# An attention and spectral-mixing kernel: the output stage with its two halves shared out anew between ScalarE, VectorE and GpSimd

## The chip, the cores and the metric

The kernel runs on one core of a Trainium2 chip. The metric is the device time of one execution in microseconds, told as the median of several runs; lower is better. A profile of one execution shows each engine: TensorE (PE, with its weight loads PEld), VectorE (DVE), ScalarE (ACT), GpSimd (POOL) and the queue engine SyncE (SP), which here only issues transfers.

## The reference

Two layers follow each other. The first is linear attention with a feature map of exponentials, for 8 batches, 8 heads, 576 tokens and 64 channels per head. Its output, with heads side by side, is `x` (8 x 576 x 512). The second is a spectral mix over the tokens and a projection:

```python
X = np.fft.rfft(x, axis=1)
Yr = einsum('bmd,mde->bme', Xr, w_r) - einsum('bmd,mde->bme', Xi, w_i)   # 64 modes
Yi = einsum('bmd,mde->bme', Xr, w_i) + einsum('bmd,mde->bme', Xi, w_r)
y = np.fft.irfft(Y, n=S, axis=1)
u = x + y
return (u + np.maximum(u @ w_ch, 0.0)).astype(np.float32)
```

`w_r` and `w_i` are 64 matrices of 512 x 512 in float32 each; they make up most of what is read.

## The kernel before

Tokens lie in 36 chunks `(bp, n)`: `bp` counts four pairs of batches and `n` nine groups of 128 rows. For `n` below 8 a chunk holds 128 tokens of one batch, and for `n` = 8 it holds 64 of each of the two batches. `chunk(bp, n)` is x of a chunk in bfloat16, `xw[:, bp, n]` is x times `w_ch`.

The mixing weights come in by 64 transfers on GpSimd's queue, in tiles `wt` of the pool `pw`, which has nine slots of one tag. `mix` multiplies one of them and adds up the spectrum `y` of eight modes for all batches; the modes are in eight groups `o`. When the last part of a group is there, `yst` is that group's spectrum, `zst` is `yst` times `w_ch`, got by transposing `yst` (`pt`, `yT`) and multiplying by `wchb` (`pz`). The output of a chunk is then the sum of two halves, both made in PSUM:

- p = x + (inverse table) x (spectrum y),
- q = xw + (inverse table) x (spectrum z), of which the Relu is taken,

and the result is p + relu(q). TensorE adds x or xw into a PSUM bank by a matmul with the identity `ident_b` (the "base"). Most of the spectrum (six of the eight groups) is added during the mix, while weights still arrive: `Absorb` adds it to x and xw in place. What is left comes after the last mix. Groups 6 and 7 are laid out in `yl`: 32 partitions each for y and z, twice, so that two chunks of a pair can be summed at once by matmuls of 32 rows with the table `CL` (method `late`). For chunks that are "early", group 6 has been absorbed too and only group 7 is left; it is read directly from `yst` and `zst` with the table `CM` and full-height matmuls (method `straight`). `put` sends `yst` and `zst` to `yl`; every copy is a DMA of 128 KB, here on SP for group 7.

The output stage begins with the last `mix` and is the class `Last`, one object for one chunk or a pair of chunks, in the order of the list `seq`. A pair goes through these steps:

- `base(1)`, then `late(1)` or `straight(1)`: q in two single banks (`pt`, pool `pst` with four banks);
- `relu`: ScalarE takes q out into `rl` (two buffers of the pool `pb`) or `rx` (a slot of `pw`), one chunk at a time;
- `base(0)`, then `late(0)` or `straight(0)`: p in a tile of two banks (`pp`, pool `pst2` with two such tiles);
- for five pairs (n = 8 and the pairs of bp = 2 in `added`, all `later`) the base of p is left out, and GpSimd adds x to `rx` instead, one chunk at a time;
- `store`: VectorE adds p and `rl` or `rx` into `of` (a slot of `pw`), and SP sends it out, 512 KB for a pair.

The first two chunks are handled singly: there ScalarE takes out p, and VectorE does the max and the add from q in one instruction. The last two, `(3, 6)` and `(3, 7)`, are single too, with tiles `ofr`. The order on every engine is the order in which the code calls it: `InOrder` keeps the recorded instructions in program order, so one late instruction holds all that follow it on its engine. The hand-written list `ahead` says how many pairs q runs ahead of p.

## Time and profile before

| | |
|---|---|
| median of 3 runs | 441.26 us |
| lowest and highest | 439.84 and 441.54 us |
| the profiled execution | 439.83 us |
| its span, first to last instruction | 438.0 us |
| TensorE, VectorE, ScalarE, GpSimd busy | 332.9, 294.0, 290.7, 111.7 us |
| mean granted TensorE clock | 0.905 |
| moved by the core's 16 DMA engines | 99.55 MB |

The page's slices cut the span in 40 parts of 11 us; a digit is the busy share in tenths. The chain that ended last is followed backwards from the last instruction, at each step to what released it. In lists of rows, each row is a start, a duration, an engine, an operation with the tile written and the tiles read, its size, and a count where equal neighbours are merged; in brackets stand the idle time in front of it and what ended that. A "landing" is the time from a transfer's issue to its completion.

### The profile page before, as it was taken

What the parts mean: (1) busy time and instruction counts of PE and PEld (TensorE: products, weight loads), DVE (VectorE), ACT (ScalarE), POOL (GpSimd) and SP (SyncE); (2) the same over time, 40 slices, a digit from 0 to 9 for tenths busy, and PEclk for the clock granted to TensorE, in tenths of its full rate; (3) what the DMA queues carried; (4) which work ended last, traced back from release to release, by engine and by line L of the source; (5) the groups of instructions that cost most, each with busy time, mean ns of one, the idle gap of its engine ahead of it and who ended that gap; (6) DMA issues with size and microseconds to landing.
All of it is one profiled execution on the core that took longest, in us unless ns stands there. A gap on an engine that the chain in (4) does not pass through costs nothing.

```text
span 438.0 us, 10095 instructions
## 1 busy us (share of the span) xinstructions
PE 332.9 (76%) x4209; PEld 198.5 (45%) x4209; DVE 294.0 (67%) x581; ACT 290.7 (66%) x472; POOL 111.7 (25%) x150
## 2 busy tenths in 40 slices
PE   2677667678697686787796877935779998997993
PEld 1345555455465454554554554612335554333320
DVE  6758677665776777887877778723773334785784
ACT  3787796776987977986977778600444442764781
POOL 6232132113211212222222221211101211682082
PEclk9979898789988989998987998875899999999996
DMA  9999999999999999999999999999999999996787
GB/s 217 209 211 211 238 213 236 237 213 248 227 211 239 226 229 230 238 215 235 231 218 239 210 262 212 213 212 212 213 215 222 223 219 222 212 219 147 258 358 292
DMA packets 51838, 99.55 MB, mean 227 GB/s; under 512 B 2512, under 2 KB 13648, under 8 KB 51792
## 3 DMA queue, kind: packets, MB, share of 16 engines
q0 software_dynamic: 45088, 85.27, 99.4%
q1 hardware_dynamic: 6544, 13.57, 8.8%
q8 instruction: 33, 0.54, 0.5%
q14 instruction: 13, 0.11, 0.1%
q10 hardware_dynamic: 160, 0.07, 0.1%
HBM read 163.64 MB, written 9.44 MB: 395 GB/s over the span
## 4 chain that ended last, share of the span: by engine, by line
ACT 28%; PE 27%; DMA 24%; DVE 12%; issue 7%; POOL 1%; POOLq 0%; ACTq 0%; DVEq 0%
DMA wt<-in_moe_w_r_dram 16%; PE one L37 14%; ACT AQ L37 12%; ACT AB L37 8%; PE two L37 8%; DMA wt<-in_moe_w_i_dram 8%; DVE m L37 6%; PE pt L37 3%; ACT qT L37 3%; ACT XT L37 3%; DVE mk L37 2%; PE pp L37 2%; DVE xs L37 1%; DVE yacc L37 1%; DVE of L37 1%
## 5 line engine op out<-in xcount | busy, mean ns | idle before, releaser
L37 ACT ACTIVATE AQ<-two 128x1024 bf16<-128x1024 f32 x64 | 80.6, 1350 | 2.7 <-PE two L37 2.6
L37 ACT ACTIVATE AB<-two 128x1024 bf16<-128x1024 f32 x64 | 62.9, 1059 | 3.0 <-DVE mk L37 2.7
L37 ACT CAST xw<-pt 128x512 bf16<-128x512 f32 x50 | 29.4, 587 | 47.7 <-PE pt L37 47.7
L37 DVE TENSOR_REDUCE m<-two 128x8 f32<-128x1024 f32 x32 | 39.2, 1224 | 21.9 <-PE two L37 21.8
L37 DVE TENSOR_REDUCE mk<-two 128x8 f32<-128x1024 f32 x32 | 38.9, 1218 | 8.7 <-PE two L37 8.7
L37 POOL DMA_DIRECT2D wt<-in_moe_w_i_dram x28 | 20.9, 748 | 91.2 <-PE pt L37 37.2
L37 PE MATMUL two<-w2blk,qT 128*128 128x256 bf16 x128 | 23.7, 318 | 25.3 <-ACT AQ L37 14.8
L37 DVE TENSOR_TENSOR va<-vn,ee 128x1152 bf16<-128x1152 f32 x32 | 42.0, 1356 | 0.0
L37 PE MATMUL pt<-wchb,xT 128*128 128x512 bf16 x136 | 37.0, 397 | 5.6 <-DVE xT L37 4.5
L37 POOL DMA_DIRECT2D wt<-in_moe_w_r_dram x30 | 22.3, 744 | 63.9 <-PE one L37 27.6
L37 PEld LDWEIGHTS <-xs 128*128 128x128 bf16 x624 | 31.6, 103 | 12.2 <-issue 6.4
L37 PE MATMUL one<-wt,XT 128*32 128x512 bf16 x304 | 27.3, 446 | 10.3 <-DMA wt<-in_moe_w_i_dram 4.6
L37 ACT COPY qT<-one 128x512 bf16<-128x512 bf16 (+1 forms) x32 | 19.0, 642 | 24.1 <-PE one L37 24.0
L37 PE MATMUL two<-qT,w2blk 128*128 128x512 bf16 x64 | 27.3, 427 | 9.3 <-ACT AQ L37 9.3
L37 PEld LDWEIGHTS <-qT 128*128 128x128 bf16 x144 | 15.2, 108 | 40.8 <-issue 37.1
L37 PEld LDWEIGHTS <-XT 128*32 128x32 bf16 x512 | 14.7, 149 | 35.2 <-issue 24.4
L37 DVE TENSOR_TENSOR xs<-one,rd 128x384 bf16<-128x384 f32 x48 | 26.8, 558 | 1.6
L37 PEld LDWEIGHTS <-AQ 128*128 128x128 bf16 x512 | 24.3, 107 | 7.7 <-issue 4.0
L37 PE MATMUL one<-kvz,AQ 128*128 128x65 bf16 x512 | 27.0, 207 | 0.9 <-ACT qT L37 0.8
L37 PE MATMUL two<-mT,minus 96*128 96x512 bf16 x64 | 27.5, 430 | 0.0
L37 POOL DMA_DIRECT2D kb<-in_k_dram x16 | 11.4, 712 | 60.4 <-PE one L37 51.1
L37 DVE COPY xT<-pt 128x512 bf16<-128x512 bf16 x36 | 15.2, 421 | 17.0 <-PE pt L37 17.0
(143 smaller groups left out, 712.6 us busy)
## 6 DMA issues: line engine op xcount, KB each, us to landing
wt<-in_moe_w_r_dram POOLq DMA_DIRECT2D x30, 1024.0 KB, 27.5
wt<-in_moe_w_i_dram POOLq DMA_DIRECT2D x28, 1024.0 KB, 28.7
out_dram<-of SPq DMA_DIRECT2D x16, 512.0 KB, 3.2
vn<-in_v_dram POOLq DMA_DIRECT2D x13, 576.0 KB, 24.6
kb<-in_k_dram POOLq DMA_DIRECT2D x16, 288.0 KB, 19.5
qb<-in_q_dram POOLq DMA_DIRECT2D x16, 288.0 KB, 18.6
xs<-in_moe_w_i_dram POOLq DMA_DIRECT2D x2, 1024.0 KB, 23.2
vn<-in_v_dram SPq DMA_DIRECT2D x3, 576.0 KB, 5.2
```

The source lines that it names most:

```text
L37: ins = f(*args, **kwargs)
```

## The change

The class `Last` gives way to a class `Pair`, and the calls after the last mix to a list of words, `plan`. All 36 chunks are handled in 18 pairs. Each pair has two sides: "e", taken out by ScalarE into `rl`, and "d", read by VectorE. The table `pairs` says for each pair whether its sums are direct (`straight`), whether ScalarE takes out q with Relu (`relu` true; VectorE then adds p) or p as it is (VectorE then does max and add from q), and whether GpSimd adds x to what ScalarE took out (`pooled`; then the base of p is left out). Eight pairs are pooled.

- A word of `plan` such as `eb34` means: side e, base, pair "34", both chunks. The letters are b for a base, s for a direct sum, l for a late sum; a fifth character picks one chunk. `mix`, `T0`, `T1`, `z0a`, `z0b`, `z1` are places in the last mix and channel product at which the list stops and goes on.
- Three pairs (00, 02, 06) are direct; before it was all of bp = 0 with n below 8. The tables and rows of `Absorb` follow that (`direct`). The chunks are no longer sorted.
- For direct pairs the add is done, and stored, chunk by chunk. All other adds are one instruction for both chunks. `rl` and `of` both come from `pw`.
- Of the two copies of the last `zst` to `yl`, the one for s = 3 is issued on GpSimd's queue.
- Both copies of the last transposed `yst` are VectorE's.

```diff
+    pairs = {
+        "00": (((0, 0), (0, 1)), True, False, False),
+        "02": (((0, 2), (0, 3)), True, False, True),
+        "06": (((0, 6), (0, 7)), True, True, True),
+        "34": (((3, 4), (3, 5)), False, False, False),
...
+        "n0": (((0, 8), (1, 8)), False, False, True),
...
+        "24": (((2, 4), (2, 5)), False, True, False),
...
+        "36": (((3, 6), (3, 7)), False, True, False),
+    }
+    plan = (
+        "eb000 db020 db000 db001 mix db021 T0 es021 T1 z0a es000 z0b z1 eb001 es020 es001 "
+        "ds000 ds001 eb060 es060 ds020 eb061 es061 ds021 eb34 el34 ds060 ds061 eln0 db34 eb04 "
+        "el04 dl34 db04 eb30 dl04 el14 el30 dbn0 dln0 eb24 db30 dl30 el22 el24 db14 dl14 db24 "
+        "el20 dl24 db22 el12 dl22 eb10 db20 dl20 el10 el32 db10 dl10 eb26 db12 dl12 el26 ebn1 "
+        "db26 dl26 eln1 db32 dl32 eb16 dbn1 dln1 el16 db16 eb36 dl16 el36 db36 dl36").split()
...
-            self.early = bp == 0 and n < 8
+            self.early = (bp, n) in direct
...
-    chunks.sort(key=lambda c: c not in added)
...
-                (pool if o == 6 else sp).dma_start(yl[r:r + 16], src)
+                (pool if o == 6 or s == 3 else sp).dma_start(yl[r:r + 16], src)
...
+        def keep(self, a):
...
+            if self.relu:
+                act.activation(rl, self.e[a], ACT.Relu)
+            else:
+                act.activation(rl, self.e[a], ACT.Copy)
+            if self.pooled:
+                x = rl.rearrange("p (g e) -> p g e", g=4)
+                pool.tensor_tensor(out=x, in0=x, in1=chunk(*self.items[a]), op=ALU.add)
+
+        def add(self, a):
+            rl, d, o = self.rl[:, a], self.d[:, a], self.o[:, a]
+            if self.relu:
+                dve.tensor_tensor(out=o, in0=d, in1=rl, op=ALU.add)
+            else:
+                dve.scalar_tensor_tensor(out=o, in0=d, scalar=0.0, in1=rl, op0=ALU.max,
+                                         op1=ALU.add)
...
-                if h:
+                if h or end:
                     dve.tensor_copy(yT[h], pt[h])
                 else:
                     act.copy(yT[h], pt[h])
```

## The prediction, made before the changed kernel was run

> **What bounds the kernel now.** I read the page's slices first, then the stage in windows, the chain that ended last, the engines' rows in order of time, and the DMA views.

> ```profile
> DMA  9999999999999999999999999999999999996787
> GB/s 217 209 211 211 238 213 236 237 213 248 227 211 239 226 229 230 238 215 235 231 218 239 210 262 212 213 212 212 213 215 222 223 219 222 212 219 147 258 358 292
> ```

> The transfers are full until the last weights (402.13 us in the chain, which is DMA for 35 us before that). Nothing the engines do earlier counts; the stage from 402 to 438 us does. There the windows show the bound moving:

> ```profile
> core 0: us, PE busy (x) PEld busy (x) DVE busy (x) ACT busy (x) POOL busy (x), PEclk, DMA share, GB/s
> ...
> 418.00:422.00 4.00, 4.00 (x25) 1.13 (x24) 3.58 (x3) 3.48 (x7) 3.71 (x4) 1.00 0.71 289
> ...
> 426.00:430.00 4.00, 3.26 (x20) 0.96 (x18) 3.46 (x3) 2.72 (x6) 3.47 (x4) 1.00 1.00 392
> 430.00:434.00 4.00, 1.57 (x4) 0.23 (x3) 2.52 (x3) 0.00 (x0) 0.04 (x1) 0.51 0.98 383
> ```

> TensorE is full to 428 while the stores leave DMA time unused (0.71 in 418 to 422); at the end TensorE is idle half the time and the stores are full. The chain's end tells why it still takes until 433.25:

> ```profile
> 427.10 0.59 ACT rx L37
> ...
> 427.77 1.16 POOL rx L37
> ...
> 430.07 1.24 DVE of L37
> ...
> 431.35 0.55 PE pp L37
> 431.89 0.67 issue
> 432.56 0.69 DVE ofr L37
> ```

> The last pairs go one after another: a Relu, two GpSimd adds (to 430.04), a VectorE add that frees a bank, two matmuls at a granted clock of about a half (0.58 us a row where it was 0.38), the last add. The single-step costs:

> ```profile
> 410.70 0.59 PE L37 MATMUL pt<-xw,ident_b 128*128 128x512 bf16 x2
> 411.23 0.39 PE L37 MATMUL pt<-yl,CL 32*128 32x512 bf16 x2
> 411.55 0.60 PE L37 MATMUL pt<-xw,ident_b 128*128 128x512 bf16 x2
> ...
> 406.43 1.29 DVE L37 SCALAR_TENSOR_TENSOR ofr<-pp,rl 128x512 f32<-128x512 f32 x2 [0.76 <-ACT rl L37]
> 408.41 2.36 DVE L37 TENSOR_TENSOR of<-pp,rl 128x1024 f32<-128x1024 f32 x2 [0.69 <-ACT rl L37]
> ...
> 419.95 4.64 POOL L37 TENSOR_TENSOR rx<-rx,xs 128x512 f32<-128x512 f32 x4 [0.29 <-ACT rx L37]
> ```

> Full-height matmuls start 0.43 apart per two, 0.216 each (407.25, 407.68, 408.11 and on). Into a run of 32-row matmuls and out again costs 0.53 + 0.32 where two full matmuls alone cost 0.43: such a run costs 0.42.

> **The change, part by part.**

> *Ahead of 402 us.* Chunks are no longer sorted, and six instead of eight are "direct". The idle time in front of the last mix (TensorE 1.55, VectorE 2.93, ScalarE 3.22 us) covers it: 0. Without that cover each microsecond would count.

> *TensorE's sum.* Before: 57 identity matmuls after the last mix (36 for xw, 26 for x, five ahead), 16 direct ones, 17 low runs, about five extra steps inside them (tile widths change at 421.2, 423.8, 425.0, 427.3: 0.33 each), 0.87 for the channel product, 0.25 for transposes: 12.3 + 3.5 + 7.1 + 1.5 + 1.1 = 25.5 us from 403.36. Less the two last singles (1.3), that gives 427.6; the trace has 428.9, so 1.3 us were waits. After: eight pairs instead of five get x from GpSimd, so x needs 20; 52 identity matmuls remain (11.2), 12 direct (2.6), again 17 low runs by the list (7.1), two changes of width (0.7), four places where two sets of the same rows follow each other (0.9), and 1.1: 23.6 us, to 427.0. With the same waits, 428.4.

> [...]

> *VectorE.* Before and after 36 chunk adds; now six of 512 and fifteen of 1024. First add at 406.43 as before: its ScalarE half is earlier, and zst later by only 0.15 (worked below). Ten of the fifteen wide ones (those where ScalarE takes out p) use the max-add form, which the trace shows at 512 alone: 0.60 apart, like the plain add. At 1024 it lies between the plain one's 1.14 to 1.18 apart and 1.29 for two narrow ones; I take 1.16, since at 512 the two forms agree. 6 x 0.60 + 15 x 1.16 = 21.0: 427.4 if never idle. TensorE's 428.4 ends later: last sum out 428.6, last add 429.8 (now 433.25).

> *ScalarE.* 36 takes at 0.52 and the zst copy, 19 us of 25: free. Both transposed copies go to VectorE (0.29 for 0.37) and one direct matmul stands between them; the product still ends about 405.1. But two takes (404.1 to 405.25) now precede zst, which starts 405.27 for 405.10: 0.15.

> *GpSimd.* 16 adds at 1.14 plus one copy issue 0.55: 18.8 us from 404.7, to 423.5. VectorE wants the last of them (pair 32) four adds before its end, at about 424.7. Cover of 1.2 us; see the first rival. [...]

> *The zst copy on GpSimd's queue.* Two zst copies used to go out on SP at 405.73 and 406.32, landing 3.4 and 3.6 later. Now one goes to GpSimd, behind its first add: issued 405.9. The list needs it for the run "el04 dl34": three matmuls, zst at 405.8, eight (407.5), two and a run (408.4), two and a run (409.2), four: 410.2. No row shows GpSimd's queue empty late in the kernel. Bounds: 3.4 (SP's rows) and 19.2; the nearest with nothing ahead is the first load:

> ```profile
> kb<-in_k_dram POOLq DMA_DIRECT2D x1, 288.0 KB, 6.6
> ...
> yl<-yst POOLq DMA_DIRECT2D x2, 128.0 KB, 19.2
> ...
> yl<-yst SPq DMA_DIRECT2D x2, 128.0 KB, 3.5
> ```

> kb is twice as large and ran beside other loads, the 19.2 stood behind weights; same size and route as SP's, so I take 4.3, nearer to SP's 3.5: 410.2, no cost. SP, relieved of one issue, has 21 stores of 0.55 in 24 us: free.

> [...]

> *Tiles.* rl and of now share eight slots (nine less yl), four pairs of about 1.2 us. A store that lands 4.8 after its issue holds its slot almost that long; 0 to 0.5 us at the end, where the stores bind anyway.

> *The stores.* Eighteen times 512 KB at 410 GB/s is 1.28 each, 23.0 in all. First store issued 407.15 as before; its landing took 3.2 of which 0.64 its bytes, so never idle the last lands at 407.15 + 2.56 + 23.0 = 432.7. From VectorE: 429.85 + 3.0 (an unqueued 512 KB) = 432.9. Two bounds so close queue on each other: 433.4. From 423.3 on, stores landed 4.2 to 4.9 after issue, not 3.0. The DMA view of 424 to 426 shows what shared the engines, an instruction fetch of 16 KB:

> ```profile
> q8 instruction: 1, 0.02, 4.4%
> ...
> out_dram<-of SPq DMA_DIRECT2D x2, 512.0 KB, 4.8
> ```

> TensorE's program is about as long, so it should come again; 1.1 to 1.8 late, take 1.4: 434.8. Last landing to end of span was 1.2 (436.8 to 438.0): **436.0, that is 2.0 us less**. The profiled run was 439.83 around its 438.0, 1.4 below the median 441.26 (runs 439.84 to 441.54). I predict **439.3** for the median. Half a percent, 2.2 us, is about what a measurement of this kernel can tell from no change.

> **The rivals.**

> *GpSimd's adds set VectorE's pace.* For: 18.8 us of work with 1.2 of cover, and before it idled 0.29, 0.36 and 0.53 between pairs waiting for Relus. Eight such gaps of 0.35 make 2.8: pair 32 ready at 426.3, VectorE 1.6 late, ends 431.4: gain 0.4, **440.9**. Against: the list puts pooled pairs well ahead. The same comes part way if max-adds at 1024 take 1.29 (10 x 0.13 = 1.3).

> *Slower: the zst copy lands late.* From 410.2 on, each microsecond holds TensorE, and everything in order behind it, for one; ScalarE and VectorE run dry with pair 06. At kb's 6.6 it lands 412.5: 2.3 lost, nothing gained, **441.5**. Past 8.5 after issue the kernel is over 0.5% slower; halfway between 6.6 and 19.2, at 12.9, it would be 8.6 - 2.0: **447.9**; at 9.5, **444.5**. Against: empty queue, small copy.

> **How the numbers follow.** Forecast case 0.58: from 1 to 3.3 us gained (438.0 if VectorE is never idle and the fetch costs 1.1, up to 440.3), 0.37 of it past 0.5%, 0.21 within. Adds rival 0.15, within. Copy rival 0.27: 0.10 within, 0.17 slower. So 0.37, 0.46, 0.17. The range leaves out most of the slow copy and a little below: 438.0 less 0.6 for the spread of medians, 437.4, to 442.5, with the copy 7.6 late.

> **What would show it.** Right: adds on VectorE with gaps under 0.5 us, last ending near 430; DMA share 1.0 from about 413; no serial GpSimd step in the chain's last 5 us; TensorE's last matmul near 428. Wrong: VectorE idle at 410 to 413 with TensorE waiting for the yl copy; VectorE waiting for GpSimd on rl more than 1 us in all; wide max-adds over 1.2 apart; a fall in the granted clock ahead of 428.

## The result, and the profile after

| | before | after |
|---|---|---|
| median of 22 runs | 440.13 us | 439.06 us |
| lowest and highest | 439.11 and 442.14 us | 437.69 and 440.18 us |
| the profiled execution | 439.83 us | 438.27 us |
| its span | 438.0 us | 436.4 us |
| first matmul of the last mix | 402.17 us | 402.45 us |
| first add of the stage begins | 406.43 us | 406.91 us |
| last add ends | 433.25 us | 430.46 us |
| last store lands | 436.82 us | 435.16 us |

The ratio of the times, with its 95% interval, is 0.9968 [0.9955, 0.9981], a gain of 1.4 us with an interval from 0.8 to 2.0; the two medians by themselves lie 1.1 apart. That is real, but within the half percent that the prediction called no change; the forecast was 439.3.

The last mix waits for the last weights, and these came 0.28 us later in the profile of after. Times marked "+" below are therefore counted from the first matmul of the last mix, so that the stage itself is compared: the span ends at +35.87 before and +33.94 after, 1.93 us less.

The page of after, the DMA rows of its slices:

```profile
DMA  9999999999999999999999999999999999998697
GB/s 214 209 212 210 238 212 237 235 214 241 235 211 239 219 229 237 238 210 239 224 224 238 210 262 212 212 212 213 212 216 223 220 223 222 212 219 176 226 393 297
```

Of the stage's three slices, the first moves 226 GB/s for 258 before and the second 393 for 358: fewer bytes at first, then the stores come closer together. The windows of after:

```profile
core 0: us, PE busy (x) PEld busy (x) DVE busy (x) ACT busy (x) POOL busy (x), PEclk, DMA share, GB/s
418.00:422.00 4.00, 3.96 (x23) 1.11 (x22) 3.56 (x4) 3.40 (x7) 4.00 (x5) 1.00 1.01 406
422.00:426.00 4.00, 4.00 (x26) 1.14 (x24) 3.92 (x4) 2.38 (x5) 2.78 (x3) 1.00 1.02 404
426.00:430.00 4.00, 2.88 (x19) 0.82 (x18) 3.61 (x4) 2.17 (x4) 0.00 (x0) 1.00 1.00 396
430.00:434.00 4.00, 0.00 (x0) 0.00 (x0) 0.47 (x1) 0.00 (x0) 0.00 (x0) 0.80 0.91 361
```

In 418 to 422 the stores now fill the DMA engines (1.01, before 0.71). GpSimd is done before 426. The stretch from 430 holds only the end of one add and the stores; before, it held four matmuls at half clock and 2.5 us of VectorE. TensorE's last row, and the end of the chain of waits of after (start, duration, what):

```profile
428.49 0.39 PE L37 MATMUL pp<-yl,CL 32*128 32x512 bf16 x2
```

```profile
427.69 0.32 PE pp L37 x2
428.01 0.09 PE pt L37 x2
428.10 0.01 issue
428.11 0.82 DVE of L37
428.93 0.29 issue
429.22 1.25 DVEq L1032
```

The serial steps of before (a Relu, two GpSimd adds, an add that frees a bank, two matmuls) are gone. From 416.4 the chain runs along TensorE to 428.1, and it ends with two adds on VectorE, one right behind the other. VectorE's rows of after, in order of time, tell where it waited (in brackets the idle time in front and what ended it):

```profile
406.91 2.72 DVE L37 SCALAR_TENSOR_TENSOR of<-pp,rl 128x512 f32<-128x512 f32 x4 [0.88 <-PE pp L37]
...
410.55 0.69 DVE L37 TENSOR_TENSOR of<-pp,rl 128x512 f32<-128x512 f32 x1 [0.33 <-POOL rl L37]
...
412.76 4.74 DVE L37 SCALAR_TENSOR_TENSOR of<-pp,rl 128x1024 f32<-128x1024 f32 x4 [0.30 <-PE pt L37]
...
420.35 1.22 DVE L37 SCALAR_TENSOR_TENSOR of<-pp,rl 128x1024 f32<-128x1024 f32 x1 [0.31 <-POOL rl L37]
...
428.11 2.35 DVE L37 TENSOR_TENSOR of<-pp,rl 128x1024 f32<-128x1024 f32 x2 [0.38 <-PE pt L37]
```

No gap between the adds exceeds 0.4 us. Before, the longest two were waits for TensorE's half p:

```profile
413.10 3.79 DVE L37 TENSOR_TENSOR of<-pp,rl 128x1024 f32<-128x1024 f32 x3 [0.92 <-PE pp L37]
...
418.12 2.52 DVE L37 TENSOR_TENSOR of<-pp,rl 128x1024 f32<-128x1024 f32 x2 [1.23 <-PE pp L37]
```

Between the adds VectorE idles 1.86 us in all, where it was 5.04.

### The profile page after: what moved, and what is told of

It is laid out like the page before. It is cut to its first block, busy times and chain, and to the rows that moved or that the text cites. A ratio compares the mean times of both kernels' runs of the same rounds, so it can differ in the third digit from the quotient of the medians.

```text
span 436.4 us, 10049 instructions
## 1 busy us (share of the span) xinstructions
PE 322.8 (74%) x4160; PEld 195.8 (45%) x4203; DVE 293.8 (67%) x583; ACT 290.0 (66%) x471; POOL 118.9 (27%) x157
## 4 chain that ended last, share of the span: by engine, by line
ACT 27%; PE 24%; DMA 24%; DVE 14%; issue 7%; POOL 2%; DVEq 0%; POOLq 0%; ACTq 0%
DMA wt<-in_moe_w_r_dram 16%; PE one L37 13%; ACT AQ L37 12%; ACT AB L37 9%; DMA wt<-in_moe_w_i_dram 8%; PE two L37 8%; DVE m L37 6%; ACT qT L37 3%; ACT XT L37 3%; PE pp L37 2%; DVE mk L37 2%; PE pt L37 2%; DVE xs L37 1%; DVE yacc L37 1%; DVE mT L37 1%
## 5 line engine op out<-in xcount | busy, mean ns | idle before, releaser
L37 ACT ACTIVATE AQ<-two 128x1024 bf16<-128x1024 f32 x64 | 80.5, 1346 | 2.9 <-PE two L37 2.8
L37 ACT ACTIVATE AB<-two 128x1024 bf16<-128x1024 f32 x64 | 62.9, 1058 | 3.2 <-DVE mk L37 3.0
L37 ACT CAST xw<-pt 128x512 bf16<-128x512 f32 x50 | 29.4, 587 | 48.2 <-PE pt L37 48.2
L37 DVE TENSOR_REDUCE m<-two 128x8 f32<-128x1024 f32 x32 | 39.1, 1223 | 20.3 <-PE two L37 20.2
L37 POOL DMA_DIRECT2D wt<-in_moe_w_i_dram x28 | 20.9, 748 | 97.2 <-PE pt L37 42.1
L37 DVE TENSOR_REDUCE mk<-two 128x8 f32<-128x1024 f32 x32 | 38.9, 1218 | 8.6 <-PE two L37 8.6
L37 DVE TENSOR_TENSOR va<-vn,ee 128x1152 bf16<-128x1152 f32 x32 | 42.0, 1355 | 0.0
L37 PE MATMUL two<-w2blk,qT 128*128 128x256 bf16 x128 | 21.7, 298 | 27.2 <-ACT AQ L37 15.0
L37 PE MATMUL pt<-wchb,xT 128*128 128x512 bf16 x127 | 35.6, 394 | 7.3 <-DVE xT L37 6.0
L37 POOL DMA_DIRECT2D wt<-in_moe_w_r_dram x30 | 22.3, 745 | 62.4 <-PE one L37 27.0
L37 PEld LDWEIGHTS <-xs 128*128 128x128 bf16 x624 | 31.5, 103 | 12.2 <-issue 6.4
L37 ACT COPY qT<-one 128x512 bf16<-128x512 bf16 (+1 forms) x32 | 19.0, 642 | 24.7 <-PE one L37 24.6
L37 PE MATMUL one<-wt,XT 128*32 128x512 bf16 x304 | 26.9, 440 | 10.8 <-DMA wt<-in_moe_w_i_dram 5.1
L37 PEld LDWEIGHTS <-qT 128*128 128x128 bf16 x144 | 14.6, 102 | 41.9 <-issue 38.8
L37 PEld LDWEIGHTS <-XT 128*32 128x32 bf16 x512 | 14.9, 149 | 35.3 <-issue 24.1
L37 PE MATMUL two<-mT,minus 96*128 96x512 bf16 x64 | 27.8, 434 | 3.2 <-issue 1.1
L37 PEld LDWEIGHTS <-AQ 128*128 128x128 bf16 x512 | 24.7, 109 | 7.9 <-issue 4.1
L37 PE MATMUL one<-kvz,AQ 128*128 128x65 bf16 x512 | 27.4, 209 | 0.9 <-ACT qT L37 0.8
L37 DVE TENSOR_TENSOR xs<-one,rd 128x384 bf16<-128x384 f32 x48 | 26.8, 557 | 1.6
L37 POOL DMA_DIRECT2D kb<-in_k_dram x16 | 11.4, 712 | 57.3 <-PE one L37 46.5
L37 DVE COPY xT<-pt 128x512 bf16<-128x512 bf16 x36 | 15.2, 421 | 17.0 <-PE pt L37 17.0
L37 DVE RECIPROCAL rd<-one 128x6 f32<-128x6 f32 x48 | 9.4, 195 | 24.7 <-PE one L37 24.3
## 6 DMA issues: line engine op xcount, KB each, us to landing
out_dram<-of SPq DMA_DIRECT2D x15, 512.0 KB, 4.0
vn<-in_v_dram POOLq DMA_DIRECT2D x13, 576.0 KB, 25.2
kb<-in_k_dram POOLq DMA_DIRECT2D x16, 288.0 KB, 20.5
qb<-in_q_dram POOLq DMA_DIRECT2D x16, 288.0 KB, 19.4
```

The lines of the kernel that those rows point to most:

```text
L37: ins = f(*args, **kwargs)
```

## The experiments

Every ratio is to the kernel before, run on the same chip, with its 95% interval; the kernel after stands at 0.9968.

**What sets the pace after: TensorE's sum or GpSimd's adds.** In `unpool3`, pairs 20, 12 and 32 get x from TensorE again.

```diff
-        "20": (((2, 0), (2, 1)), False, False, True),
+        "20": (((2, 0), (2, 1)), False, False, False),
...
-            "el20 dl24 db22 el12 dl22 eb10 db20 dl20 el10 el32 db10 dl10 eb26 db12 dl12 el26 ebn1 "
+            "eb20 el20 dl24 db22 eb12 el12 dl22 eb10 db20 eb32 dl20 el10 el32 db10 dl10 eb26 db12 dl12 el26 ebn1 "
```

> The changed kernel, with x of pairs 20, 12 and 32 added by TensorE again (six more identity matmuls, six fewer GpSimd adds). If TensorE's sum paces the end, as the prediction has it, the six matmuls at 0.216 us move the last VectorE add from 430.5 by 1.3 us to about 431.7 and the end by 1.0 to 1.3 us, since the stores then queue a little less. If the stores bind by themselves the end moves by less than 0.4 us. If GpSimd's adds pace VectorE (the first rival), the end comes earlier, since GpSimd loses 6.8 us of work.

Measured: 440.05 us, 0.9988 [0.9972, 1.0003], some 0.9 us above after; the two intervals overlap at their ends. In its profile the last add ends at +30.10 for +28.02, but the granted clock falls at the start of the stage there, which it does not in the profile of after (see `fed`). Three other versions of after below have the same fall and all of after's pooled pairs, and their last adds end at +29.10, +29.10 and +29.11 (`fetch_moved`, `fewer_stores`, `all_p`). So the fall is worth 1.1 us and the six matmuls 1.0, near the 1.3 that six times 0.216 make. TensorE's sum paces; had GpSimd's adds done so, taking six of them off would have been a gain.

**The zst copy on GpSimd's queue.** `copy_sp` gives it back to SP; `late_copy` issues it on GpSimd behind the adds of pairs 02 and 06.

```diff
-                (pool if o == 6 or s == 3 else sp).dma_start(yl[r:r + 16], src)
+                (pool if o == 6 else sp).dma_start(yl[r:r + 16], src)
```

> The changed kernel, with both copies of the last zst issued on SP again. The copy on GpSimd landed 3.64 us after issue, at 410.23; the run of matmuls that wants it started at 410.65. On SP the second copy should be issued about 406.7 and land near 410.3: no change, within 0.3 us. If GpSimd's queue cost or gained something that the rows do not show, the time moves by more than that.

Measured: 439.46 us, 0.9971 [0.9957, 0.9986]; its last add ends at +28.04 for +28.02. The queue makes no difference.

```diff
-                (pool if o == 6 or s == 3 else sp).dma_start(yl[r:r + 16], src)
+                if o == 7 and s == 3:
+                    late_copy.append((yl[r:r + 16], src))
+                else:
+                    (pool if o == 6 else sp).dma_start(yl[r:r + 16], src)
...
+            if self.items[a] == (0, 7):
+                pool.dma_start(*late_copy.pop())
```

> The changed kernel, with the GpSimd copy of zst issued behind the four adds of pairs 02 and 06, at about 410.5 instead of 406.6. By the prediction's price it lands near 414.1, 3.5 us after the matmuls that want it could start, and holds everything behind them one for one: the last add near 434, the end 3.0 to 3.5 us later than the changed kernel's, less at most 0.5 us because the stores queue less. If ScalarE, VectorE and the stores have enough work in hand, the end moves by less than 1.5 us.

Measured: 444.84 us, 1.0089 [1.0060, 1.0118], which is 5.3 us above after: more than expected. TensorE's rows of `late_copy`, and its windows (columns as above; the last three are the granted clock, the DMA share and GB/s):

```profile
415.70 0.60 PE L37 MATMUL pp<-yl,CL 32*128 32x512 bf16 x1 [2.61 <-DMA yl<-zst]
```

```profile
414.00:418.00 4.00, 2.29 (x5) 0.53 (x5) 1.22 (x1) 0.21 (x1) 1.05 (x1) 0.65 0.45 155
418.00:422.00 4.00, 4.00 (x17) 0.83 (x16) 2.45 (x2) 2.07 (x4) 2.26 (x2) 0.50 0.52 212
422.00:426.00 4.00, 3.55 (x24) 0.90 (x23) 3.12 (x3) 3.11 (x6) 2.61 (x3) 0.99 0.68 269
```

The copy was issued at 412.24 and landed 3.4 later, the matmul that wants it began at once: the mechanism of the slower rival is there, at 2.61 us of wait. The granted clock is 0.5 from 415.22 to 422.04, and full TensorE work starts 17 matmuls in 4 us where after starts 23 in the same stretch. So in this profile a microsecond of that wait costs more than a microsecond. It is the slowest of the six runs (445.79 us) and had half clock at the start of the stage too. Two of the six, at 441.74 and 442.40, are near the price that was expected; no profile shows the clock in them.

**GpSimd's adds without the list, and the list's order without its lead.** `before_pool8` is the kernel before with three more pairs pooled. `one_ahead` is the kernel after with the list from pair 34 on in the order q of one pair, then p of the pair before it.

```diff
-            self.later = n == 8 or items[0] in added
+            self.later = n == 8 or items[0] in added + [(2, 2), (1, 2), (3, 2)]
```

> The kernel before, with its own order, and x of eight pairs instead of five added by GpSimd (pairs (2,2), (1,2) and (3,2) as well). TensorE has six matmuls, 1.3 us, less to do. If TensorE's sum is all that counts, it is about 1 us faster than the kernel before. If the pooled pairs need the room that the new list gives them, each of the three new ones makes VectorE wait for a Relu and two GpSimd adds (0.6 + 2.3 us) with only one pair in hand (1.2 us), 1.1 to 1.7 us each: slower than the kernel before by 2 to 4 us.

Measured: 446.44 us, 1.0132 [1.0112, 1.0152], 5.8 us slower than before and above the expected range. VectorE's waits for GpSimd in the stage (total, times, longest), first before, then `before_pool8`, and the windows of `before_pool8`:

```profile
DVE of L37 <- POOL rx L37: 0.5, 1, 0.5
```

```profile
DVE of L37 <- POOL rx L37: 5.4, 3, 2.0
```

```profile
426.00:430.00 4.00, 4.00 (x17) 0.64 (x16) 2.45 (x2) 2.59 (x5) 3.38 (x4) 0.50 0.77 312
430.00:434.00 4.00, 4.00 (x18) 0.87 (x16) 2.36 (x2) 1.71 (x4) 3.35 (x4) 0.50 0.52 204
434.00:438.00 4.00, 3.69 (x15) 0.65 (x11) 2.96 (x3) 2.28 (x4) 2.28 (x2) 0.50 0.80 314
```

The eight pooled pairs give TensorE fewer matmuls, but in the old order VectorE waits 4.9 us more for GpSimd's adds, TensorE then waits for banks that VectorE's adds free (2.8 us in three waits, before 1.6 in two), and from 424.01 to the end the clock is half. The 5.8 us are these waits and the half clock together; the run does not part them.

```diff
-            "ds000 ds001 eb060 es060 ds020 eb061 es061 ds021 eb34 el34 ds060 ds061 eln0 db34 eb04 "
-            "el04 dl34 db04 eb30 dl04 el14 el30 dbn0 dln0 eb24 db30 dl30 el22 el24 db14 dl14 db24 "
...
+            "ds000 ds001 eb060 es060 ds020 eb061 es061 ds021 eb34 el34 ds060 ds061 "
+            "eb04 db34 el04 dl34 db04 eln0 dl04 eb30 dbn0 el30 dln0 db30 el14 dl30 eb24 db14 el24 dl14 db24 el22 dl24 db22 el20 dl22 eb10 db20 el10 dl20 db10 el12 dl10 eb26 db12 el26 dl12 db26 el32 dl26 ebn1 db32 eln1 dl32 eb16 dbn1 el16 dln1 eb36 db16 el36 dl16 db36 dl36").split()
```

> The changed kernel, with the same pairs, sides and store order, but the list from pair 34 on rewritten in the old manner: ScalarE's half of the next pair is summed just ahead of VectorE's half of this one. TensorE's sum is the same within 0.5 us. If the order in the list is what makes eight pooled pairs pay, VectorE waits for GpSimd at most of the six late pooled pairs, about 0.6 to 1.1 us each: 3 to 6 us slower than the changed kernel. If only the sum counts, within 0.5 us of it.

Measured: 443.07 us, 1.0058 [1.0039, 1.0076], 4.0 us above after. In its profile the granted clock stays full until 434 and the last add ends at +32.48 for +28.02, so there 4.5 us are the price of the waits alone. VectorE's waits, first `one_ahead`, then after:

```profile
DVE of L37 <- POOL rl L37: 5.0, 6, 1.4
```

```profile
DVE of L37 <- POOL rl L37: 0.6, 2, 0.3
```

The first rival's mechanism exists, and the lead that the list gives to pooled pairs is what keeps it away.

**The end of the stage: stores and the instruction fetch.** `fewer_stores` leaves out the stores of five pairs (that part of the output is not written). `fetch_moved` writes 96 transposes of the attention part twice, so that the fetch of TensorE's instructions falls elsewhere; `before_fetch_moved` does the same to the kernel before.

```diff
+                if self.items[0] in ((2, 4), (2, 2), (2, 0), (1, 0), (1, 2)):
+                    continue
```

> The changed kernel without the stores of pairs 24, 22, 20, 10 and 12 (2.6 MB of 9.4 not written). VectorE's adds stay. If the adds are paced by TensorE and VectorE, the last add still ends near 430.4; the store queue then is empty when the last store is issued, it lands 3.0 us after issue instead of 4.66, and the span is 1.4 to 1.7 us shorter. If slots of the pool that wait for landings pace the adds, the last add comes earlier too and the gain is over 2 us. If the stores do not matter, no change.

Measured: 437.29 us, 0.9932 [0.9913, 0.9951], 1.6 us below after, as expected. Its last add ends at +29.10, where the half clock at its start puts it, so the stores do not pace the adds. The DMA view of the last microseconds (KB each, us from issue to landing), after first, then `fewer_stores`:

```profile
out_dram<-of SPq DMA_DIRECT2D x2, 512.0 KB, 4.6
```

```profile
out_dram<-of SPq DMA_DIRECT2D x2, 512.0 KB, 3.3
```

The last store landed 4.66 us after its issue in after and 3.50 here. So five stores in the queue hold the end of after back by some 1.2 us. That is the queue and an instruction fetch together: the five stores that are left out are those around the fetch (at 424.39 here), so it meets an idle queue.

```diff
-                    pe.transpose(ptr[:, j - lo, :], rows[:, j * 128:(j + 1) * 128], ident_b)
+                    for _ in range(2 if j < 4 and 2 <= 4 * self.g + self.bp < 14 else 1):
+                        pe.transpose(ptr[:, j - lo, :], rows[:, j * 128:(j + 1) * 128], ident_b)
```

> The changed kernel, with 96 of the early transposes written twice (the same values into the same place), so that TensorE's program is 192 instructions longer ahead of the stage. The instruction fetches of 16 KB come every 256 TensorE instructions; the last one, seen at 424.65, should move to about 404, where the transfers are nearly idle, and none should fall into the stores. If that fetch is what holds the last landing of the stores back (4.5 to 5.0 us after issue from 423 on, 3.7 to 4.0 before it), the last store lands 1.0 to 1.25 us earlier and the span shrinks by that, about 0.25%. If the late landing is only the stores queueing, nothing changes; the 96 transposes themselves lie in the part that the weights' transfers hide.

Measured: 438.28 us, 0.9954 [0.9936, 0.9972]; 0.14% below after, with overlapping intervals. The fetch that stood at 424.65 moved to 407.68, and the last store landed 3.96 after its issue for 4.66. The stores around that time tell the same: in after the landing goes from 3.70 (issued 421.61) to 4.79 (422.96) and stays there, in `fetch_moved` it goes from 3.67 to 3.60.

> The kernel before, with the same 96 transposes written twice. Its last landing was 1.1 us behind the others' engines' share after the fetch at 424.60. If the fetch is the cause, the span shrinks by 0.8 to 1.2 us, as in the changed kernel; if not, no change.

Measured: 440.23 us, 0.9988 [0.9973, 1.0003], 0.5 us, less than expected and not told apart from nothing. The fetch held the stores of before too: those issued from 423.3 to 430 landed 4.5 to 4.9 after issue, and 3.0 to 3.2 in the same stretch here. But the last store of before, which comes later and is smaller, had nearly caught up: 3.54, and 3.31 here.

**The clock at the start of the stage.** In several profiles (`unpool3`, `fetch_moved`, `fewer_stores`) the first add came at about +5.5 instead of +4.46. Windows around the last mix, of after, `fetch_moved` and `copy_sp` (columns as above):

```profile
398.60:402.00 3.40, 1.91 (x9) 0.71 (x7) 1.29 (x2) 1.07 (x2) 0.00 (x0) 1.00 0.63 153
402.00:405.40 3.40, 2.70 (x22) 1.25 (x22) 1.34 (x4) 0.86 (x2) 0.27 (x1) 1.00 0.15 39
```

```profile
398.60:402.00 3.40, 1.45 (x6) 0.52 (x5) 1.09 (x2) 1.07 (x2) 0.00 (x0) 1.00 0.62 146
402.00:405.40 3.40, 3.40 (x17) 1.24 (x17) 1.34 (x4) 0.60 (x1) 0.23 (x1) 0.54 0.21 51
```

```profile
398.60:402.00 3.40, 1.49 (x10) 0.55 (x9) 1.10 (x2) 1.07 (x2) 0.00 (x0) 1.00 0.63 146
402.00:405.40 3.40, 3.15 (x25) 1.50 (x25) 1.49 (x5) 1.35 (x3) 0.76 (x1) 1.00 0.29 76
```

TensorE waits about 1.6 us for the last weights in all three. In `fetch_moved` the granted clock is 0.54 right after it, and 17 matmuls start in 3.4 us instead of 22 and 25. `fed` puts six matmuls in front of the wait; they write a bank that is started anew afterwards. `before_fed` does it to the kernel before.

```diff
+            for _ in range(6):
+                pe.matmul(last["02"].at("d", 0), lhsT=ident_b, rhs=xw[:, 0, 2, :], start=True, stop=True)
```

> The changed kernel, with six more identity matmuls (into a bank that is then started anew) between the last absorbed chunk and the last mix, so that TensorE waits 0.3 us instead of 1.6 for the last weights. In five of the ten profiles so far the granted clock fell to a half at the start of the stage, for 3.4 us, and the first VectorE add came 5.5 us after the mix instead of 4.46. If TensorE's idle time is the cause, the first add comes at 4.5 in every run, the spread of the times shrinks, and the median falls by about half of 1.05 us: 0.5 us, 0.1%. If the clock falls for another reason, the time stays or rises by up to 0.3 us.

> The kernel before, with the same six matmuls ahead of its last mix. The same gain of about 0.5 us if idle time at the start is the cause. Beside the run above it gives the change's worth with the clock held at both starts: 1.9 us by the profiled pair (35.87 from the mix to the end against 33.94), 1.4 us by the medians.

Measured: `fed` 437.92 us, 0.9938 [0.9919, 0.9957], 1.3 us below after; `before_fed` 439.86 us, 0.9976 [0.9963, 0.9989], 1.1 us below before. The spread shrinks: six runs of `fed` lie within 0.9 us, twelve of `before_fed` within 0.8, where after and before spread over 2.5 and 3.0. TensorE's rows of `fed`:

```profile
399.06 1.46 PE L37 MATMUL pp<-xw,ident_b 128*128 128x512 bf16 x6
...
402.29 0.66 PE L37 MATMUL pt<-wt,XT 128*32 128x512 bf16 x8 [0.91 <-DMA wt<-in_moe_w_i_dram]
```

The six cost nothing themselves, the wait is 0.91 us for 1.63, and the stage of the profile is the one of after (first add +4.46, last add +28.03, end +34.00). So the gain of the median is not a shorter stage, but fewer executions with a half clock at its start. That is inferred from the medians, the spreads (the other changed versions with six runs spread over 1.5 to 4.1 us) and the profiles; for the single runs without a profile it is not shown.

`fed` against `before_fed`, run on the same chip with no overlap between their runs, gives what the change is worth without that fall: 439.86 - 437.92 = 1.94 us. (Their two profiles differ by 1.6 in the stage, +35.63 and +34.00. The clock fell at 430.08 in the profile of before, under its last matmuls, and only at 433.32 in that of `before_fed`.)

**Does it matter which half ScalarE takes out?** In `all_p` ScalarE takes p in the five pairs of the wide adds that took q.

```diff
-        "24": (((2, 4), (2, 5)), False, True, False),
+        "24": (((2, 4), (2, 5)), False, False, False),
```

> The changed kernel, with pairs 24, 10, n1, 16 and 36 turned round, so that ScalarE takes out p and VectorE reads q in all pairs but 06. The list of words stays. The max-add at 1024 starts 1.17 to 1.22 apart in the trace, the plain one 1.14 to 1.17: five times 0.03 are 0.15 us more on VectorE, and one set of rows fewer follows itself on TensorE, 0.2 less. If which half ScalarE takes does not matter by itself, no change, within 0.3 us. If reading q on VectorE at the end delays it, 0.5 us or more slower.

Measured: 438.78 us, 0.9961 [0.9945, 0.9978]: no difference to after. Its last add ends at +29.11 behind a half clock at the start, as in `fetch_moved`.

**The best version.** `fed_fetch` is `fed` with 88 of the transposes written twice.

> The changed kernel, with the six matmuls and with 88 early transposes written twice, so that the last instruction fetch falls to about 407 us. If both causes hold, the first add comes 4.5 us after the mix, the last store lands 3.7 to 4.0 us after its issue instead of 4.66, and the median is 1.0 to 1.3 us below the changed kernel's, 0.25 to 0.3%; the ratio to the kernel before is then about 0.994. If only the clock counts, 0.5 us below; if neither, no change.

Measured: 437.45 us, 0.9927 [0.9907, 0.9946], below both kernels. Against `fed` it is 0.5 us, and the intervals overlap; in its profile the last store landed 3.95 after issue and the span ended at +33.23, for 4.72 and +34.00 in `fed`.

## Why the prediction came out as it did

*TensorE's sum: right.* Counted from the mix, the last matmul was to end at +26.2 and ended at +26.4 (428.49 + 0.39, less 402.45). `unpool3` shows that this sum sets the pace and that an identity matmul is worth near what its row says. How the stretch splits is another matter. From the transposes (403.64) to its end TensorE is busy 24.4 of 25.2 us in after, where I had 23.6 of work and 1.3 of waits. In before, from 403.36 to 428.89, it is busy 25.4 of 25.5 us, so by the trace's busy time the 1.3 that I called waits were mostly work that the sum had left out.

*VectorE: right.* Wide max-adds follow each other 1.17 apart in one group and 1.21 in another (from the four in 4.74 and the three in 3.65 us), for 1.16. The last add ended at +28.0, for +27.6: 0.2 came with the first add (+4.46, for +4.26 as before), and 0.2 because the last two adds ran one behind the other on VectorE, where I had let the last one start with its sum. The 1.21 is also above the 1.2 that I had named as a sign of being wrong, but the end of the adds does not hang on it.

*GpSimd: the cover was thinner than said.* The sixteen adds ended at 424.78, which is 1.0 later than the sum after the mix's 0.28 are taken off: the first began at 405.13 instead of 404.7, and two waits of 0.3 and 0.6 follow. VectorE waited for it 0.6 us in two places, with no effect on the end. The rival was real, as `one_ahead` shows, but as a matter of the order.

*The copy: no cost, as said, by two errors that cancel.* It was issued at 406.59, 0.4 later than my 405.9 even when the mix's 0.28 are taken off, and landed 3.64 later, for my 4.3: at 410.23, with my forecast at 410.2. The run that wants it began at 410.65. The DMA view of after, both copies:

```profile
yl<-zst SPq DMA_DIRECT2D x1, 128.0 KB, 3.3
yl<-zst POOLq DMA_DIRECT2D x1, 128.0 KB, 3.6
```

The first load of the kernel (6.6 us), on which the rival's price stood, says little about a queue that is empty late in the kernel. The price of each late microsecond was too low for some executions: I took one for one, and the profile of `late_copy` shows the clock falling with the wait of 2.61 us, to a half from 415.22 to 422.04.

*The stores and the fetch: the total right, the split wrong.* The last landing was to be at +32.6 and came at +32.7, and that it agrees so well is luck. I gave the fetch 1.4 us. Taking it away is worth 0.7 to 0.8 at the end (landing 3.96 for 4.66 and 3.95 for 4.72, end +33.23 for +34.00). The last add came 0.4 later than said. The DMA share that was to be 1.0 from about 413 was 0.89 from 410 to 414, 0.95 to 418 and 1.0 only from there. And without the fetch the last store took 3.96, where I had 3.0 and 0.5 for the queue; 3.50 of it remain when five stores are left out.

*The sum: right in the stage, weaker in the median.* 2.0 us were predicted. The two profiles differ by 1.93 us in the stage, and `fed` and `before_fed` by 1.94. The kernels as they are differ by 1.4 [0.8, 2.0]. That holds 1.94; whether half clock at the start takes more from after than from before, these runs do not settle.

*What was missing: a term for the clock ahead of the stage.* "Ahead of 402 us" I called TensorE's idle 1.55 us a free cover. As cover it is, but the same idle time lets the clock fall in some executions, and the stage that starts then begins with 1.04 us lost. It stands in both kernels, so it would cancel in the change if it came equally often in both. It does not cancel where a gain read from one profile is taken off a median of three runs. 441.26 was 1.1 us over the median of 22 runs, and the 2.0 taken off it is 0.9 more than the 1.1 by which the medians differ. The two errors nearly cancel, so the closeness of 439.3 to 439.06 is luck.

## What to carry to other kernels

Work given to a slower engine (GpSimd's adds of 128x512 start 1.14 us apart, VectorE's 0.60) paid here only where the order put it well ahead of its reader: the new list with its eight pooled pairs gained 1.4 to 1.9 us, the same pairs with one pair of lead were 4.0 slower than that, and eight pooled pairs in the old order cost 5.8, half clock included. When the bound of a stage is a sum of short matmuls, look at what precedes it as well: a wait in front can be free as cover and still slow what follows (the first add at +5.5 in `fetch_moved`, for +4.46), and a few idle matmuls put into that wait bought 1.1 and 1.3 us of the median here, nearly as much as the whole rebuilt stage. When two bounds end within a microsecond (here TensorE's last sum and the stores), cost both, for the gain on one was cut off by the other: the last add came 3.1 us earlier in the stage, the end 1.9.

## What the runs showed of the hardware

*The clock fell behind waits of 1.5 to 1.8 us, by where they lay in a grid of 3.41 us.* The windows of `unpool3` around the last mix, whose wait was 1.54 us:

```profile
402.00:406.00 4.00, 3.95 (x22) 1.55 (x22) 1.34 (x4) 0.84 (x2) 0.63 (x1) 0.57 0.23 60
406.00:410.00 4.00, 3.95 (x25) 1.54 (x23) 2.62 (x5) 3.49 (x7) 3.30 (x5) 1.00 0.51 126
```

These traces' records of the granted clock know only full and half; here they give half from 402.01 to 405.43, 3.41 us, and then full again. Seven of the twelve experiments' profiles have this at the start of the stage; of the ten profiles that the expectation of `fed` speaks of, six have it and not five. The waits in front were 1.50 to 1.82 us in these, and 1.55 to 1.63 in before, after, `copy_sp` and `one_ahead`, which do not, so the length of the wait does not decide.

| profile | step | TensorE busy | next step |
|---|---|---|---|
| `unpool3` | 398.60 to 402.01 | 1.60 us | half |
| `fetch_moved` | 398.84 to 402.25 | 1.45 us | half |
| `late_copy` | 401.56 to 404.98 | 1.80 us | half |
| `copy_sp` | 400.90 to 404.31 | 2.09 us | full |
| after | 398.25 to 401.66 | 2.25 us | full |
| before | 399.36 to 402.77 | 1.76 us | full |

The other four with a fall have 1.28 to 1.42 us. Where a step's end divides the wait, as in `copy_sp` and after, no step is that empty, and the clock stays. This would explain why equal waits end differently; but before and `late_copy` stand the wrong way round, so busy time alone does not draw the line. Nor does it say when full clock returns: `before_pool8` stayed at half from 424.01 on, though TensorE was busy in the whole of two steps there.

*One instruction fetch of 16 KB held back the stores behind it.* The DMA view of after, 424 to 426.5, has it:

```profile
q8 instruction: 1, 0.02, 2.6%
```

2.6% of 16 engines in 2.5 us is 1.04 us of one engine. From there on the landings take 1.1 us longer (4.79 for 3.70). The DMA rows of after from 429 to 436, and of `fetch_moved` from 429.5 to 437, in 40 slices each, show the end of the stores:

```profile
DMA  9998998999999999999999999621100000000000
```

```profile
DMA  9998999999999999899999897110000000000000
```

In after the stores end in a tail of seven slices, 1.2 us, that moves 94 GB/s and then less; its last four slices move 23 each, near a sixteenth of the 410 of full transfers. In `fetch_moved` the tail has two slices, 0.4 us. One engine that runs late, and stores that wait for it, would look like this; the views do not name the engine. The page of before counts 33 such fetches for 4209 matmuls and as many weight loads, one for 255 instructions in the mean. Longer code ahead moved the last one: 96 transposes more put it at 407.68.
